# The boot of an attention and two-layer kernel: another order of fetches, passes and engines

## The chip, the cores and the metric

The program runs on one core of one Trainium2 chip. The metric is the device time of one execution in microseconds (us). A core has TensorE (PE; its weight loads are shown apart as PEld), VectorE (DVE), ScalarE (ACT), GpSimd (POOL) and SyncE (SP), which here issues the transfers. The engines run apart and wait for one another by semaphores.

## What is computed

The reference, cut to what matters: a linear attention with decay over 4 batches, 8 heads, 768 positions and head size 64; then a layer with a softmax-weighted activation and a norm; then a layer with a cosine.

```python
gamma = 1.0 - 2.0 ** (-5.0 - np.arange(H))
for t in range(S):
    state = gamma * state + einsum('bhd,bhe->bhde', k[:, :, t], v[:, :, t])
    y[:, :, t] = (1 / sqrt(D)) * einsum('bhd,bhde->bhe', q[:, :, t], state)
x = y.transpose(0, 2, 1, 3).reshape(B * S, H * D)         # 3072 tokens x 512
h = x @ w_in                                              # 512 x 1024
e = exp(h - max(h)); solu = h * e / (sum(e) + 1e-09)
ln = (solu - mean(solu)) / sqrt(var(solu) + 1e-06) * g_ln
x2 = ln @ w_out                                           # 1024 x 512
h2 = x2 @ w_in2; out = (h2 * cos(h2)) @ w_out2            # 512 x 2048 x 512
```

## The kernel before

**Attention.** The sequence is cut into 12 chunks of 64 positions, two batches at a time: 24 steps, each of which yields one tile of 128 tokens. `load` (L224) fetches for a step `dk` (k and q, 512 KB), `sv` (v and k, 512 KB) and `g` (decay factors, 128 KB), each into one of three buffers. GpSimd scales v by `kf` (L246). `attn(scores, outs)` (L281) then runs on TensorE: scores `sc` of one step (L257), the state `S` (L265) and the output `y` (L278) of the step before it. VectorE masks the scores to `M` (L311) and scales y by g to `x` (L324); ScalarE copies the state to `s` (L319).

**First layer.** Products are made in three passes of fp32r: each operand is split into a high part and the rest, and high x high, low x high and high x low are added up. `split` (L330) makes `xh` on ScalarE and `xl` on VectorE. The weights come as 64-bit words; `words` (L343) fetches a tile of them (`raw`) and turns it into fp32: one step on ScalarE (L353), three on VectorE (L357, L361, L366), a fourth one for the low word (L373). `w1` (L390) ends in `w1h` on ScalarE (L398) and `w1l` on VectorE (L401). w_in comes in five tiles: column half 0 in rows 0, 1 and 2 to 3 (two narrow tiles, 128x512, and a wide one, 128x1024), column half 1 in two wide tiles. `mm1(n, c)` (L456) makes h of token tile n, column half c, in 4 x 3 products (L471). `norm` (L478) reduces and scales h; `transp` and `mm2` (L527, L551) carry on to w_out, whose four tiles are converted by `o1` (L408).

**Order.** Nothing runs in the order in which it is written. `add` records an operation with its engine, cost, buffers and a due time; `Plan.order` (L97) replays engines and one wire (`MBUS`, in MB per us) and puts the operations out one after another; TensorE may pick among the next `LOOK` operations, the others by due time. The constants on top (L52 to L65) steer that. Each engine then runs its own instructions strictly in that order. `record` (L786) opens with the boot: tiles of w_in, the loads and the first attention steps by hand, then mm1 of tiles 0 and 1, and from tile 2 on a regular sequence of mm1, one attention step per tile, and w_out's conversion.

Of the kernel before, what the change touches and what calls it, by code (L numbers as in the profile page):

```python
# [22 lines left out]
C = 64  # L23
NI = S // C
# [40 lines left out]
B_LOAD = 0.0  # L65


class Plan:
# [28 lines left out]
    def order(self):  # L97
# [18 lines left out]
        at, sat, out = 0, 0, []  # L116
# [3 lines left out]
        while len(out) < n:  # L120
# [34 lines left out]
            free[e] = end  # L155
# [17 lines left out]
class Body:  # L173
# [48 lines left out]


    def load(self, n):  # L224
        bp, i = self.steps[n]
# [22 lines left out]
        self.add("POOL", 1.12, scale, w=[("v", sl)])  # L248
# [94 lines left out]
    def words(self, key, src, pool, slot, apart, wide=2):  # L343
# [40 lines left out]
        self.add("DVE", 0.15 + 0.55 * wide, low, r=[wk] if apart else [rk], w=[rk] if apart else [wk], bias=b)  # L384
# [5 lines left out]
    def w1(self, c, k, wide, slot):  # L390

        key = ("w1", c, k)
        rk, wk = self.words(key, self.pair("w_in1", k, slice(c * 1024, (c + 1) * 1024), wide), "boot", slot, True, wide)
# [6 lines left out]
        def low():  # L400
# [5 lines left out]
                 bias=self.bias)  # L406
# [144 lines left out]
    def mm2(self, g, p, look=1):  # L551
        for e in range(2):
            def go(e=e):
                if e == 0:
                    self.new("pst", ("y1", g), [128, 2, 256], F32, "y1")
                ds = slice((2 * p + e) * 128, (2 * p + e + 1) * 128)
                m = 0
                for j in range(K1):
                    lh, ll = self.t["lth", g, j // 2], self.t["ltl", g, j // 2]
                    for w, a in ((self.t["o1h"], lh), (self.t["o1l"], lh), (self.t["o1h"], ll)):  # L560
                        self.nc.tensor.matmul(out=self.t["y1", g][:, e], lhsT=w[:, j, ds], rhs=a[:, j % 2],  # L561
                                              start=(m == 0), stop=(m == 3 * K1 - 1))
                        m += 1
            self.add("PE", 2.88, go, r=[(w, f) for w in ("lth", "ltl") for f in range(4)]
# [432 lines left out]
```

## Time and profile before

| | us |
|---|---|
| median of three runs | 897.58 |
| lowest and highest | 897.24, 900.46 |
| the profiled execution, its own time | 900.29 |
| its span | 898.5 |
| TensorE busy | 876.3 (98%) |
| VectorE busy | 580.6 (65%) |
| ScalarE busy | 408.7 (45%) |
| GpSimd busy | 100.1 (11%) |

The span runs from the first to the last instruction on the core; what lies around it is in the profiled execution's time too. A busy TensorE is not TensorE at its peak: the records tell that it worked on something, and the granted clock beside it tells at which rate. The share of the whole span says little about a stage of it, so the rows further down are by stage.

### The profile page before, as it was taken

Reading aid. Unit: us, or ns where it says so; the run is one execution under the profiler, and the core shown is the slowest. Engines: PE = TensorE matmul, PEld = TensorE weight load, DVE = VectorE, ACT = ScalarE, POOL = GpSimd, SP = SyncE. Lnnn points to the kernel's source line nnn. Section 1 sums busy time; section 2 is a strip of 40 time slices with the busy share of each in tenths; the row PEclk is TensorE's granted clock in tenths of the full one; section 3 lists DMA queues with packets and bytes.
Section 4 is the critical chain, followed back from the end, with each engine's and each line's share of the span. In section 5 each row is a group of like instructions: output and inputs, shape, how many; then the busy total and the mean of one; then the engine's idle time right before and its main releaser. Section 6 shows DMA issues by size and latency. Waiting matters only on the chain.

```text
span 898.5 us, 16993 instructions
## 1 busy us (share of the span) xinstructions
PE 876.3 (98%) x7168; PEld 751.6 (84%) x7168; DVE 580.6 (65%) x849; ACT 408.7 (45%) x630; POOL 100.1 (11%) x200
## 2 busy tenths in 40 slices
PE   5799999999999999999999999999999999999997
PEld 4588899999999999988888888888888888888886
DVE  5899866658577565566666566556655665557553
ACT  3387665445454466453343344334433443334332
POOL 1254422223221221000000000000000000000000
PEclk9999999999999999999999999999999999999999
DMA  9766545676765264231030002000200020011002
GB/s 349 276 216 207 172 140 183 209 256 207 256 204 180 95 195 144 72 110 43 1 94 0 1 24 71 1 1 24 71 1 0 24 71 1 0 46 26 1 1 47
DMA packets 35852, 90.29 MB, mean 100 GB/s; under 512 B 4032, under 2 KB 13248, under 8 KB 35776
## 3 DMA queue, kind: packets, MB, share of 16 engines
q1 hardware_dynamic: 35344, 89.14, 30.4%
q8 instruction: 56, 0.92, 0.4%
q14 instruction: 20, 0.16, 0.1%
q10 hardware_dynamic: 432, 0.06, 0.0%
HBM read 68.22 MB, written 20.97 MB: 99 GB/s over the span
## 4 chain that ended last, share of the span: by engine, by line
PE 93%; DVE 4%; DMA 1%; issue 1%; ACT 0%; POOL 0%; SPq 0%; DVEq 0%; POOLq 0%
PE h L671 29%; PE acc L732 29%; PE y L561 16%; PE h L471 13%; PE tr L533 2%; PE sc L257 1%; PE y L278 1%; PE S L265 1%; DVE wt L366 1%; DMA sv<-vk_dram 1%; DVE raw L373 1%; DVE w1l L401 0%; DVE wt L357 0%; DVE wt L361 0%; DVE u L493 0%
## 5 line engine op out<-in xcount | busy, mean ns | idle before, releaser
L671 PE MATMUL h<-yh,w2h 128*128 128x512 f32 x384 | 149.5, 389 | 0.0
L671 PE MATMUL h<-yh,w2l 128*128 128x512 f32 x384 | 149.4, 389 | 0.0
L671 PE MATMUL h<-yl,w2h 128*128 128x512 f32 x384 | 149.4, 389 | 0.0
L732 PE MATMUL acc<-o2h,gh 128*128 128x512 f32 x384 | 149.4, 389 | 0.0
L732 PE MATMUL acc<-o2h,gl 128*128 128x512 f32 x384 | 149.4, 389 | 0.0
L732 PE MATMUL acc<-o2l,gh 128*128 128x512 f32 x384 | 149.4, 389 | 0.0
L692 ACT ACTIVATE r<-r,hp 128x512 f32<-128x512 f32 x96 | 69.5, 724 | 159.8 <-DVE r L689 159.8
L561 PE MATMUL y<-lth,o1h 128*128 128x256 f32 x384 | 110.0, 287 | 0.5 <-issue 0.5
L695 DVE TENSOR_TENSOR r<-r,h 128x512 f32<-128x512 f32 x96 | 65.9, 687 | 66.8 <-ACT r L692 66.8
L561 PE MATMUL y<-lth,o1l 128*128 128x256 f32 x384 | 108.6, 283 | 0.0
L561 PE MATMUL y<-ltl,o1h 128*128 128x256 f32 x384 | 108.6, 283 | 0.0
L681 DVE SCALAR_TENSOR_TENSOR r<-ki,h 128x512 f32<-128x512 int32 x96 | 65.9, 686 | 64.1 <-ACT ki L676 63.8
L703 DVE TENSOR_TENSOR gl<-r,gh 128x512 fp32r<-128x512 f32 x96 | 66.3, 690 | 45.8 <-ACT gh L699 45.6
L676 ACT ACTIVATE ki<-h 128x512 int32<-128x512 f32 x96 | 57.1, 595 | 79.6 <-PE h L671 79.6
L699 ACT ACTIVATE gh<-r 128x512 fp32r<-128x512 f32 x96 | 60.5, 630 | 55.3 <-DVE r L695 55.2
L671 PEld LDWEIGHTS h<-yl,w2h 128*128 128x128 f32 x384 | 72.1, 188 | 15.1
L732 PEld LDWEIGHTS acc<-o2h,gh 128*128 128x128 f32 x384 | 72.1, 188 | 15.0
L732 PEld LDWEIGHTS acc<-o2l,gh 128*128 128x128 f32 x384 | 72.0, 188 | 15.0
L732 PEld LDWEIGHTS acc<-o2h,gl 128*128 128x128 f32 x384 | 72.1, 188 | 14.9
L671 PEld LDWEIGHTS h<-yh,w2l 128*128 128x128 f32 x384 | 72.1, 188 | 14.8
L671 PEld LDWEIGHTS h<-yh,w2h 128*128 128x128 f32 x384 | 72.1, 188 | 14.8
L471 PE MATMUL h<-w1h,xh 128*128 128x512 f32 x192 | 78.8, 411 | 2.1 <-ACT w1h L398 1.4
(72 smaller groups left out, 1481.4 us busy)
## 6 DMA issues: line engine op xcount, KB each, us to landing
dk<-kq_dram SPq DMA_DIRECT2D x24, 512.0 KB, 4.6
sv<-vk_dram SPq DMA_DIRECT2D x24, 512.0 KB, 5.7
raw<-w_out_dram SPq DMA_DIRECT2D x12, 1024.0 KB, 6.8
raw<-w_in_dram SPq DMA_DIRECT2D x11, 1024.0 KB, 8.1
y1d<-ys SPq DMA_DIRECT2D x24, 256.0 KB, 2.7
yt<-y1d SPq DMA_DIRECT2D x24, 256.0 KB, 3.6
out_dram<-o SPq DMA_DIRECT2D x48, 128.0 KB, 2.4
kept_in<-wt SPq DMA_DIRECT2D x8, 512.0 KB, 4.7
```

The source lines that it names most:

```text
L257: self.nc.tensor.matmul(out=sc[r, j], lhsT=dk[r, 0, j], rhs=dk[r, 1, j], start=True, stop=True)
L471: self.nc.tensor.matmul(out=h[:, c], lhsT=a[:, k], rhs=w[:, k, cs], start=(k + m == 0), stop=(k == KD - 1 and m == 2))
L533: self.nc.tensor.transpose(out=tr[:, e, t * 128:(t + 1) * 128], in_=self.t["u", 2 * g + t].rearrange("p c f -> p (c f)")[:, j * 128:(j + 1 ...
L561: self.nc.tensor.matmul(out=self.t["y1", g][:, e], lhsT=w[:, j, ds], rhs=a[:, j % 2], start=(m == 0), stop=(m == 3 * K1 - 1))
L671: nc.tensor.matmul(out=h, lhsT=w[:, cs], rhs=a[:, k], start=(m == 0), stop=(m == 3 * KD - 1))
L676: nc.scalar.activation(out=T["ki", n, j], in_=T["h2", n, j], func=AF.Identity, scale=INV2PI, bias=0.25)
L681: nc.vector.scalar_tensor_tensor(out=r, in0=ki, scalar=-C1, in1=T["h2", n, j], op0=ALU.mult, op1=ALU.add)
L692: nc.scalar.activation(out=T["r", n, j], in_=T["r", n, j], func=AF.Sin, bias=self.hp[:, 0:1])
L695: nc.vector.tensor_tensor(out=T["r", n, j], in0=T["r", n, j], in1=T["h2", n, j], op=ALU.mult)
L699: nc.scalar.activation(out=T["gh", n, j], in_=T["r", n, j], func=AF.Copy)
L703: nc.vector.tensor_tensor(out=T["gl", n, j], in0=T["r", n, j], in1=T["gh", n, j].bitcast(F32), op=ALU.subtract)
L732: nc.tensor.matmul(out=T["acc", n, t], lhsT=a[:, ts_], rhs=w, start=(j == 0 and m == 0), stop=(j == K2 - 1 and m == 2))
```

## The change

The constants of the plan differ; the other parts, in the order of the diff:

- `warm`: 32 products of the identity with itself, written into the buffer of h of tile 0, as the first work of TensorE.
- `load`: g lies behind v and k in one transfer of 640 KB; for the steps in `V_ACT` ScalarE scales v in four instructions, one for each pair of heads, instead of GpSimd in one.
- `words` and `w1`: the two VectorE steps on the low words get a due time that is `B_LOW` later.
- `mm1` takes a range of passes, `(0, 2)`, `(2, 3)` or all; `mm2` is recorded in four pieces per output half instead of one.
- The constants tri, kf and g_ln come in one transfer `rows`.
- The boot is a list of words, `BOOT`: `w` a tile of w_in (column half, row, width, buffer), `L` a load, `s` scores, `a` an attention step, `x` a split, `m` products (tile, column half, rows from `PARTS`, passes).

```diff
-MBUS = 0.29
+MBUS = 0.40
+SHARE = 0.7
+EASE = 0.08
+WARM = 32
+V_ACT = (0, 2, 3, 7, 11, 12, 13)
-LOOK = 4
+LOOK = 3
...
-B_O1 = 16.0
-B_KEEP = 12.0
+B_O1 = 20.0
+B_KEEP = 6.0
...
-O1_AT = (1, 2, 4, 5)
+O1_AT = (2, 3, 4, 6)
...
+B_LOW = 24.0
+JOIN = 2
+PARTS = ((0,), (1,), (2, 3), (0, 1), (0, 1, 2, 3))
+BOOT = ("w:0010 w:0111 w:1023 L:0 L:1 s:0 a w:0222 x:0 L:2 s:1 a x:1 m:00002 a m:01302 m:10402 m:00102 a m:10423 a"
+        " m:00202 w:1224 m:00423 m:01202 m:01423:done m:11403:done x:2")
...
+            if e == "POOL" and ops[i][6] == "big":
+                if free["DVE"] > start:
+                    free["DVE"] += SHARE
+                else:
+                    owed = end
+            if e == "DVE" and start < owed:
+                end += SHARE
+                owed = 0.0
+            free[e] = end - (EASE if e in ("DVE", "ACT") else 0.0)
...
+    def warm(self):
+
+        t = self.new("ps1", ("warm",), [128, 2, 512], F32, "h")
+        for i in range(WARM):
+            self.nc.tensor.matmul(out=t[:, 0, 0:128], lhsT=self.ident, rhs=self.ident, start=True, stop=True)
...
         def sv():
-            t = self.new("att", ("sv", n), [128, 2, 8, C], F32, f"sv{sl}")
-            self.nc.sync.dma_start(out=t, in_=self.a["vk"][bp, i].rearrange("p (u j s) -> p u j s", u=2, s=C))
-
-        def g():
-            t = self.new("att", ("g", n), [128, NHP, C], F32, f"g{sl}")
-            self.nc.sync.dma_start(out=t, in_=self.a["c_g"][i].rearrange("p (a t) -> p a t", t=C))
+            t = self.new("att", ("svg", n), [128, 20 * C], F32, f"sv{sl}")
+            self.nc.sync.dma_start(out=t, in_=self.a["vk"][bp, i])
...
+        def scale_act():
+            v = self.t["sv", n][:, 0].rearrange("p (a b) e -> p a (b e)", b=2)
+            for a in range(NHP):
+                self.nc.scalar.activation(out=v[:, a], in_=v[:, a], func=AF.Copy, scale=self.kf[:, i, a:a + 1])
+
+        if n in V_ACT:
+            self.add("ACT", 1.60, scale_act, w=[("v", sl)])
+        else:
+            self.add("POOL", 1.12, scale, w=[("v", sl)], name="big")
...
-        self.add("DVE", 0.15 + 0.55 * wide, low, r=[wk] if apart else [rk], w=[rk] if apart else [wk], bias=b)
+        self.add("DVE", 0.15 + 0.55 * wide, low, r=[wk] if apart else [rk], w=[rk] if apart else [wk], bias=b + late)
...
-        if n == c == 0:
-            self.split(0)
-        if c == (n > 0) and n + 1 < NS:
+        if c == 1 and 1 < n < NS - 1:
             self.split(n + 1)
...
-                    for m, (a, w) in enumerate(((xh, self.w1h), (xl, self.w1h), (xh, self.w1l))):
+                    for m, (a, w) in list(enumerate(((xh, self.w1h), (xl, self.w1h), (xh, self.w1l))))[slice(*passes)]:
...
-            self.add("PE", 2.88, go, r=[(w, f) for w in ("lth", "ltl") for f in range(4)]
-                     + [(w, j) for w in ("o1h", "o1l") for j in range(K1)] + [("pool", "pst")], w=[("y1", e)], look=look,
-                     name=f"mm2 {g},{p},{e}")
+                self.add("PE", 0.72, go, r=[("lth", f), ("ltl", f), ("pool", "pst")] + ([("y1", 0)] if e else [])
+                         + [(w, 2 * f + i) for w in ("o1h", "o1l") for i in range(2)], w=[("y1", e)], look=look,
+                         name=f"mm2 {g},{p},{e},{f}")
...
-        nc.scalar.dma_start(out=self.tri, in_=self.a["c_tri"])
-        nc.scalar.dma_start(out=self.kf, in_=self.a["c_kf"].rearrange("p (a t) -> p a t", t=NHP))
-        nc.scalar.dma_start(out=self.gcol, in_=self.a["gln"])
+        nc.scalar.dma_start(out=rows, in_=self.a["c_rows"])
...
+        self.add("PE", 9.4, self.warm, w=[("h", 0, 0), ("h", 0, 1)], name="warm")
+        for word in BOOT.split():
+            kind, *arg = word.split(":")
```

What this does to the order shows best at three places. First TensorE, from the last attention rows of step 1 to the first products of h (`h<-w1h,xh` and its kin); before:

```order
L278 MATMUL y_247<-M1_239,sv1_125 64x64 x2
L278 MATMUL y_247<-dk1_123,s1_211 64x64 x16
L471 MATMUL h_294<-w1h_111,xh0_216 128x512
L471 MATMUL h_294<-w1h_111,xl0_243 128x512
L471 MATMUL h_294<-w1l_112,xh0_216 128x512
L471 MATMUL h_294<-w1h_111,xh0_216 128x512
L471 MATMUL h_294<-w1h_111,xl0_243 128x512
L471 MATMUL h_294<-w1l_112,xh0_216 128x512
L257 MATMUL sc_316<-dk2_131 64x64 x16
L471 MATMUL h_294<-w1h_111,xh0_216 128x512
L471 MATMUL h_294<-w1h_111,xl0_243 128x512
```

and now:

```order
L308 MATMUL y_270<-M1_259,sv1_154 64x64 x2
L308 MATMUL y_270<-dk1_152,s1_263 64x64 x16
L499 MATMUL h_328<-w1h_107,xh0_317 128x512
L499 MATMUL h_328<-w1h_107,xl0_325 128x512
L287 MATMUL sc_335<-dk2_158 64x64 x16
L499 MATMUL h_328<-w1h_107,xh0_317 128x512
L499 MATMUL h_328<-w1h_107,xl0_325 128x512
L499 MATMUL h_328<-w1h_107,xh0_317 128x512
L499 MATMUL h_328<-w1h_107,xl0_325 128x512
L287 MATMUL sc_371<-dk0_199 64x64 x2
L308 MATMUL y_374<-M0_366,sv2_160 64x64 x2
```

The products with w1l have left this place, and the scores of step 3 and the output of step 2 follow on the products with w1h.

Second VectorE, from its first instruction on; `wt0`, `raw0` and `wt1`, `raw1` are the two narrow tiles of w_in; before:

```order
L357 TENSOR_SCALAR wt0_135<-wt0_135 128x512
L361 TENSOR_SCALAR wt0_135<-wt0_135 128x512
L366 SCALAR_TENSOR_TENSOR wt0_135<-raw0_113,wt0_135 128x512
L373 SCALAR_TENSOR_TENSOR raw0_113<-raw0_113,wt0_135 128x512
L311 TENSOR_TENSOR M0_167<-sc_146,tri_66 128x512
L401 TENSOR_TENSOR w1l_112<-raw0_113,w1h_111 128x512
L324 TENSOR_TENSOR x0_207<-y_174,g0_119 128x512
L357 TENSOR_SCALAR wt1_205<-wt1_205 128x512
L361 TENSOR_SCALAR wt1_205<-wt1_205 128x512
L366 SCALAR_TENSOR_TENSOR wt1_205<-raw1_121,wt1_205 128x512
L373 SCALAR_TENSOR_TENSOR raw1_121<-raw1_121,wt1_205 128x512
L311 TENSOR_TENSOR M1_239<-sc_220,tri_66 128x512
```

and now:

```order
L387 TENSOR_SCALAR wt0_162<-wt0_162 128x512
L391 TENSOR_SCALAR wt0_162<-wt0_162 128x512
L396 SCALAR_TENSOR_TENSOR wt0_162<-raw0_142,wt0_162 128x512
L387 TENSOR_SCALAR wt1_166<-wt1_166 128x512
L403 SCALAR_TENSOR_TENSOR raw0_142<-raw0_142,wt0_162 128x512
L391 TENSOR_SCALAR wt1_166<-wt1_166 128x512
L431 TENSOR_TENSOR w1l_108<-raw0_142,w1h_107 128x512
L396 SCALAR_TENSOR_TENSOR wt1_166<-raw1_144,wt1_166 128x512
L403 SCALAR_TENSOR_TENSOR raw1_144<-raw1_144,wt1_166 128x512
L431 TENSOR_TENSOR w1l_108<-raw1_144,w1h_107 128x512
L341 TENSOR_TENSOR M0_197<-sc_177,rows_66 128x512
L387 TENSOR_SCALAR wt1_194<-wt1_194 128x1024
```

Both narrow tiles now go ahead of the first mask M0, and the first x, seventh before, is no longer among these rows.

Third SP's queue of transfers; before:

```order
L349 DMA raw0_113<-w_in1_dram 128x1024
L230 DMA dk0_115<-kq_dram 128x1024
L234 DMA sv0_117<-vk_dram 128x1024
L238 DMA g0_119<-c_g_dram 128x256
L349 DMA raw1_121<-w_in1_dram 128x1024
L230 DMA dk1_123<-kq_dram 128x1024
L234 DMA sv1_125<-vk_dram 128x1024
L238 DMA g1_127<-c_g_dram 128x256
L349 DMA raw2_129<-w_in1_dram 128x2x1024
L230 DMA dk2_131<-kq_dram 128x1024
L234 DMA sv2_133<-vk_dram 128x1024
L238 DMA g2_137<-c_g_dram 128x256
```

and now, from the second on (the first is `raw0` as before):

```order
L379 DMA raw1_144<-w_in1_dram 128x1024
L379 DMA raw3_146<-w_in1_dram 128x2x1024
L254 DMA dk0_148<-kq_dram 128x1024
L258 DMA sv0_150<-vk_dram 128x1280
L254 DMA dk1_152<-kq_dram 128x1024
L258 DMA sv1_154<-vk_dram 128x1280
L379 DMA raw2_156<-w_in1_dram 128x2x1024
L254 DMA dk2_158<-kq_dram 128x1024
L258 DMA sv2_160<-vk_dram 128x1280
L254 DMA dk0_199<-kq_dram 128x1024
L258 DMA sv0_319<-vk_dram 128x1280
L379 DMA raw4_321<-w_in1_dram 128x2x1024
```

Two more tiles of w_in stand ahead of dk0, g has gone, and raw4 stands behind the sv that takes buffer 0 for the second time.

## Rows read from the trace of the kernel before

**Rows 1.** busy time by stage; columns: stretch, length, busy time of each engine (instructions), clock, DMA

```profile
0.00:6.98 6.98, 0.00 (x1) 0.00 (x1) 0.73 (x2) 1.94 (x2) 0.76 (x8) 1.00 0.71 216
6.98:19.25 12.27, 9.20 (x225) 8.56 (x225) 8.15 (x13) 4.78 (x7) 2.92 (x3) 0.89 1.03 407
19.25:39.74 20.49, 14.50 (x323) 10.88 (x321) 20.11 (x22) 6.99 (x8) 4.88 (x4) 0.98 0.76 277
39.74:47.72 7.98, 7.55 (x145) 6.02 (x145) 4.79 (x7) 4.25 (x6) 0.66 (x3) 0.79 0.85 315
47.72:111.90 64.18, 64.04 (x1163) 53.09 (x1164) 59.26 (x77) 47.44 (x72) 34.69 (x73) 1.00 0.59 195
111.90:893.40 781.50, 780.97 (x5319) 673.02 (x5317) 487.13 (x730) 342.92 (x537) 56.20 (x111) 1.00 0.25 80
```

**Rows 2.** waits of TensorE up to 48 us; columns: in total, times, longest

```profile
PE sc L257 <- DMA dk<-kq_dram: 7.0, 1, 7.0
...
PE h L471 <- DVE w1l L401: 4.5, 3, 1.9
...
PE y L278 <- DVE M L311: 2.0, 1, 2.0
...
PE h L471 <- ACT w1h L398: 1.4, 1, 1.4
...
PE h L471 <- DVE u L493: 0.4, 1, 0.4
```

**Rows 3.** busy time from VectorE's first instruction to its last w1l

```profile
6.20:39.70 33.50, 23.70 (x544) 19.45 (x544) 28.95 (x36) 11.76 (x15) 7.80 (x6) 0.95 0.87 328
```

**Rows 4.** timeline of VectorE; columns: start, length, line, what, [idle before <- releaser]

```profile
6.68 0.43 DVE L361 TENSOR_SCALAR wt<-wt 128x512 int32<-128x512 int32 x1
...
7.14 0.69 DVE L366 SCALAR_TENSOR_TENSOR wt<-raw,wt 128x512 int32<-128x512 int32 x1
...
12.83 1.14 DVE L361 TENSOR_SCALAR wt<-wt 128x512 int32<-128x512 int32 x1
...
21.41 1.23 DVE L366 SCALAR_TENSOR_TENSOR wt<-raw,wt 128x1024 int32<-128x1024 int32 x1
...
27.60 1.95 DVE L366 SCALAR_TENSOR_TENSOR wt<-raw,wt 128x1024 int32<-128x1024 int32 x1
...
41.19 1.23 DVE L487 TENSOR_REDUCE sm<-h 128x1 f32<-128x1024 f32 x1 [0.90 <-PE h L471]
...
45.30 1.23 DVE L487 TENSOR_REDUCE sm<-h 128x1 f32<-128x1024 f32 x1 [2.29 <-PE h L471]
```

**Rows 5.** timeline of TensorE: the scores of steps 0 and 2

```profile
6.98 1.97 PE L257 MATMUL sc<-dk 64*64 64x64 f32 x32 [6.98 <-DMA dk<-kq_dram]
...
21.20 1.15 PE L257 MATMUL sc<-dk 64*64 64x64 f32 x32
```

**Rows 6.** chain of waits; columns: start, length, what

```profile
39.74 5.54 PE h L471 x16
...
53.45 0.20 PE sc L257 x2
...
55.48 5.67 PE h L471 x24
...
112.47 0.87 PE tr L533 x8
```

**Rows 7.** timeline of POOL: the identity, and v of steps 0 and 3

```profile
1.07 0.29 POOL masks.py:199 TENSOR_SCALAR_AFFINE_SELECT ident<-ident 128x128 f32<-128x128 f32 x1
...
8.45 1.04 POOL L246 TENSOR_TENSOR sv<-sv,kf 128x512 f32<-128x512 f32 x1 [7.08 <-DMA sv<-vk_dram]
...
27.16 1.30 POOL L246 TENSOR_TENSOR sv<-sv,kf 128x512 f32<-128x512 f32 x1 [7.48 <-DMA sv<-vk_dram]
```

**Rows 8.** timeline of ScalarE: one narrow and one wide instruction

```profile
7.86 0.63 ACT L398 ACTIVATE w1h<-wt 128x512 fp32r<-128x512 f32 x1 [1.68 <-DVE wt L366]
...
17.96 1.12 ACT L353 ACTIVATE wt<-raw 128x1024 f32<-128x1024 f32 x1
```

More of the change, by code (lines that the diff above doesn't have):

```diff
@@ L340, in split, with words @@
         self.add("DVE", 0.70, low, r=[("x", n % RING), ("xh", n % 2)], w=[("xl", n % 2)])
-    def words(self, key, src, pool, slot, apart, wide=2):
+    def words(self, key, src, pool, slot, apart, wide=2, late=0.0):
         rk = ("raw", pool, slot)
@@ L392, in w1 @@
         key = ("w1", c, k)
-        rk, wk = self.words(key, self.pair("w_in1", k, slice(c * 1024, (c + 1) * 1024), wide), "boot", slot, True, wide)
+        rk, wk = self.words(key, self.pair("w_in1", k, slice(c * 1024, (c + 1) * 1024), wide), "boot", slot, True, wide, B_LOW)
         cs = slice(c * 512, (c + 1) * 512)
@@ L464, in go @@
             def go(ks=ks):
-                if c == 0 and ks[0] == 0:
+                if ("h", n) not in self.t:
                     self.new(pool, ("h", n), [128, 2, 512], F32, "h")
@@ L469, in go @@
                 for k in ks:
-                    for m, (a, w) in enumerate(((xh, self.w1h), (xl, self.w1h), (xh, self.w1l))):
+                    for m, (a, w) in list(enumerate(((xh, self.w1h), (xl, self.w1h), (xh, self.w1l))))[slice(*passes)]:
                         self.nc.tensor.matmul(out=h[:, c], lhsT=a[:, k], rhs=w[:, k, cs], start=(k + m == 0),
                                               stop=(k == KD - 1 and m == 2))
-            self.add("PE", 0.68 * len(ks) + 0.03, go, r=[("xh", n % 2), ("xl", n % 2), ("pool", pool)]
-                     + [(w, c, k) for w in ("w1h", "w1l") for k in ks], w=[("h", hb, c)], look=look, name=f"mm1 {n},{c}")
-        if c == 1:
+            need = [("xh", n % 2), ("pool", pool)] + ([("xl", n % 2)] if passes[0] < 2 and passes[1] > 1 else [])
+            need += [("w1h", c, k) for k in ks if passes[0] < 2] + [("w1l", c, k) for k in ks if passes[1] > 2]
+            self.add("PE", 0.227 * len(ks) * (passes[1] - passes[0]) + 0.03, go, r=need, w=[("h", hb, c)], look=look,
+                     name=f"mm1 {n},{c},{passes}")
+        if c == 1 and done:
             self.norm(n, hb)
@@ L762, in setup @@
         self.hp = hp.tile([128, 120], F32, name="hp")
-        self.tri = const.tile([128, C], F32, name="tri")
-        self.kf = const.tile([128, NI, NHP], F32, name="kf")
-        self.gcol = const.tile([128, K1], F32, name="gcol")
+        rows = const.tile([128, C + NI * NHP + K1], F32, name="rows")
+        self.tri = rows[:, 0:C]
+        self.kf = rows[:, C:C + NI * NHP].rearrange("p (a t) -> p a t", t=NHP)
+        self.gcol = rows[:, C + NI * NHP:]
         self.mhalf = const.tile([128, 8], F32, name="mhalf")
@@ L832, in record @@
         oq = [(0, "stg", 0), (1, "stg", 1), (2, "boot2", 0), (3, "stg", 0)]
-        self.mm1(0, 1, ((0, 1), (2, 3)), look=look)
-        for n in range(1, 2 * EARLY):
+        for n in range(2 * EARLY):
             if n > 1:
@@ L926, in body @@
 @with_exitstack
-def body(ctx: ExitStack, tc: tile.TileContext, kq, vk, c_g, c_tri, c_kf, w_in1, w_out1, gln, w_in2, w_out2, out):
-    b = Body(ctx, tc, kq=kq, vk=vk, c_g=c_g, c_tri=c_tri, c_kf=c_kf, w_in1=w_in1, w_out1=w_out1, gln=gln,
-             w_in2=w_in2, w_out2=w_out2, out=out)
+def body(ctx: ExitStack, tc: tile.TileContext, kq, vk, c_rows, w_in1, w_out1, w_in2, w_out2, out):
+    b = Body(ctx, tc, kq=kq, vk=vk, c_rows=c_rows, w_in1=w_in1, w_out1=w_out1, w_in2=w_in2, w_out2=w_out2, out=out)
     b.setup()
```

85 lines of the change are left out of this document (41 added, 44 removed).

## The prediction

> **What bounds the kernel now.** I read the busy time by stage first [rows 1]. From 47.72 us on TensorE is busy 64.04 of 64.18 us, and then 780.97 of 781.50: nothing is to be had there. Before that it is idle 6.98 + 3.07 + 5.99 + 0.43 = 16.5 us. I call 47.72, where the first product of h for token tile 2 starts, the mark; what follows it is a dense stream, so the kernel ends earlier by as much as the mark comes earlier, plus the TensorE work that is already done at the mark and was not before. The waits of TensorE [rows 2] say what the idle time is: 7.0 until the first dk has landed, 4.5 for the low part of w_in1 (w1l, on VectorE), 2.0 for a mask, 1.4 for w1h, and 0.4 at the mark itself. Last, VectorE in the stretch that ends with the last w1l (39.68): it is busy 28.95 of 33.5 us [rows 3]. So VectorE, converting w_in1 from 64-bit words, is the bound of the boot, and every w1l in it holds the three-pass products behind.
>
> **The passes split, and VectorE's new order.** The same five tiles of w_in1 are converted with the same 25 instructions. Before, TensorE needed a tile's w1l for its third product; now the xh and xl products against w1h run for tiles 0 and 1 first, and the w1l products later. So w1l is no longer what TensorE waits for, until the last one. VectorE's count from its start (6.2) to the last w1l: 35 instructions before, 36 now (five masks and two xl as before, four x instead of three). Its pure work before is 28.95 less the stretch that POOL causes. While POOL scales v, a VectorE instruction next to it takes 1.14 instead of 0.43, or 1.95 instead of 1.23 [rows 4]; there are four such in this stretch, two of which are shown, together 2.5 us. So 28.95 - 2.5 = 26.4, and with one x more (0.69 long, 0.6 of it before the next starts) 27.0.
>
> What it waits for now. Before M0 stand the ten instructions of the two narrow tiles: 2 x (2 x 0.43 + 3 x 0.69) = 5.9 us [rows 4], so it reaches M0 at 12.1. M0 needs sc0, and sc0 needs dk0 and the end of the idle products (both below: 11.1 and 11.9); sc0 takes 1.15 us at the faster pace [rows 5]; M0 can start at 13.2, a wait of 1.1. Nothing later is late by my count: x0 needs y0, which runs after sc1 (dk1 lands at 14.1) from 15.3 to 16.4, and VectorE reaches x0 at 17.1; x1 needs y1 at about 19.2, reached at 21. Of POOL's products three (steps 1, 4, 5) still lie in the stretch: 3 x 0.7 = 2.1 (0 to 3). Sum: 6.2 + 27.0 + 1.1 + 2.1 = 36.4 for the last w1l, 3.3 earlier than 39.7. Bounds: 34.3 without any stretch, 39.7 if all is eaten.
>
> TensorE between: the first product needs xl0, which VectorE finishes at 6.2 + 5.9 + 1.1 + 6.2 = 19.4 (eight instructions from M0 to xl0, six of at most 0.69 and two of 1.23 [rows 4], 6.6, less some 0.4 by which records overlap). Up to the last w1l it has 34 products of 0.236 (24 in 5.67) = 8.0, sc2 with 1.15, and the attention steps (3,2), (4,3), (5,4) with 2.03 each (55.48 - 53.45) = 6.1 [rows 5, 6]: 15.3 us, done at 34.7 if never held. That leaves 1.7 us of cover under VectorE. Behind the last w1l come 14 products (3.3), the attention step (6,5) (2.0), and the gap of 0.4 [rows 2]: 36.4 + 5.8 = 42.2 for the mark, 5.5 earlier, and with one attention step (2.03) more done than before: 7.5 us.
>
> **w_in1 fetched first.** Three tiles of it (2.10 MB) now go ahead of dk0 on SP's queue, so dk0 is behind 2.62 MB instead of 1.05. Before, sv0 had landed at 8.35 with 1.57 MB issued up to it, and the sv of step 3 at 27.1 with 8.78 MB [rows 7]: 0.385 MB per us. dk0 then lands at 8.35 + 1.05/0.385 = 11.1, four us later than before; sv0 at 12.8, sv1 at 15.9. This is the cost of the reorder, and it is already in the 1.1 us wait above. The last w_in1 tile (raw4) lands with 8.91 MB at 27.4; ScalarE's first step on it takes 1.12 [rows 8]; VectorE reaches it at about 29: no wait, with half a us of cover.
>
> **Constants, g with v.** Three constant transfers become one and 24 g transfers vanish into v's. SP's issues shrink; the bytes stay: nothing. But the buffer of v is now held until x has read g, so SP's fetch of sv for step 3 waits for x0, and raw4 and all later fetches stand behind it in SP's queue. By the times above x0 ends at 17.8, and raw4, issued then, is limited by the bytes ahead of it, not by the wait. Zero here; a us late for each us that x0 ends after some 18.5.
>
> **Idle products.** 32 products of the identity need only the identity (made from 1.07 on, in 0.29 [rows 7]). A transpose of 128 columns takes 0.109 (8 in 0.87) [rows 6]; an fp32 product has two such records, 64 in all: 7.0 us at the faster pace and 13.9 at half of it, so they end between 8.5 and 15.4. I take the middle, 11.9, because the stretch must start at the lower pace: sc0 took 1.97 before, right after idling, against 1.15 for the same 32 records later [rows 5]. They cost 0.8 against dk0 (11.1), in the 1.1 above; from 0 to 4.3. The Trainium skill (TensorE: Matmul & The Clock Gate, Part 1) has it that the default state is throttled and activity releases the throttle; the trace's two durations of sc agree. By that rule sc0 and sc1 run at the faster pace; without it sc0 would end 0.8 us later, and so would the sum.
>
> **v on ScalarE.** Seven of the 24 steps leave POOL (1.04 to 1.30 each [rows 7]) for four ScalarE instructions on 128 columns. From 1.12 for 1024 and 0.63 for 512 columns [rows 8] I take 0.14 + 0.12 = 0.26 each, 1.05 a step; at most 4 x 0.63 = 2.5. Step 0 alone is on the path: v landed at 12.8, scaled at 13.9, wanted by TensorE at 15.3: hidden, and barely so at 2.5. ScalarE has room after the mark (47.44 of 64.18 [rows 1]). The Trainium skill (ScalarE: Activation LUTs, Rules for kernel authors) budgets about 0.3 us per ACTIVATE and 0.83 ns per element; by that a step takes 1.6, an estimate from that page, and the sum is the same.
>
> **The rest.** mm2 in quarters and the planner's new constants move rows in a stretch where TensorE waits 0.14 + 0.53 us in all [rows 1]: 0, between -0.5 and +1.
>
> **Does the rest keep the lead?** VectorE's lead at the last w1l is 3.3 + 0.6 = 3.9; before, its reductions of h of tiles 0 and 1 then waited 0.9 and 2.3 us for TensorE [rows 4], which falls away: 7.1 at the mark. From the mark to 111.9 it is busy 59.26 of 64.18 [rows 1], 4.9 of slack, so it can follow. I take back 0.5. Net 7.0.
>
> **Rivals.** (1) The lead is given back: if VectorE keeps only the 3.9, because norm and w_out1 steps bunch up, the time is 897.58 - 3.9 = 893.7. For it: VectorE is at 92% after the mark. Against: fewer POOL products beside it. (2) More than forecast: no stretch and early products give a last w1l at 34.3, a lead of 9.1: 888.5. (3) The slow one: the lower clock. TensorE still has gaps (13.1 to 14.2, about 16.4 to 17.1), and before, after the waits for w1l, 16 products from 39.74 took 5.54 us instead of 3.8 [rows 6], the clock of that stage being 0.79 [rows 1]: partly the lower of its two levels, 1.2 GHz. If it is low from the first product to the last w1l, 15.3 us of work become 1.97/1.15 = 1.7 times as long: + 10.7, less 1.7 of cover, = 9.0, and the time is 899.6. If the idle products run low throughout too, M0 is 3.5 later: 903.1, slower. It turns against the change from 7.0 us of such loss on; a fall over a third of the stretch gives about 893 to 895. (4) The split does not do what it says: if tile 0's products still wait for other operands (xl0, w1h), TensorE's 34 products come late and the cover of 1.7 is gone; each us beyond that is one lost, 893 for 4 us.
>
> **The numbers.** The profiled execution took 900.29, its span 898.5 with 1.8 around it; like for like the changed kernel's would be 893.3. The three runs have a median of 897.58, 2.7 below it; 897.58 - 7.0 = 890.6. If this loss from 39.74 on is the profiled run's own, the lead is about 1.7 smaller: 892.3, inside the forecast's own range, 888.9 to 893.0. Chances: forecast 0.60, (2) 0.12, (1) and (4) 0.12, (3) in part 0.10, (3) whole 0.06. 0.5%, about what a measurement here can tell from no change, is 4.5 us: faster is below 893.1. Faster 0.60 + 0.12 = 0.72; same 0.22; slower 0.06. The range 888.0 to 895.0 leaves out (3) beyond a third and the edge of (2).
>
> **What would show it.** Right: the first sc at 11 to 12.5; VectorE without a wait over 0.5 us from M0 to the last w1l, which ends at 35 to 38; TensorE waiting for w1l once or twice, under 2 us together; the first h of tile 2 at 41 to 44 with the attention step (6,5) before it; no wait of TensorE over 1 us after that. Wrong: idle products ending after 14; a granted clock near 0.5 between 20 and 37 us; raw4's first step starting after 30; a chain after the mark that runs through VectorE to about 100, with TensorE waiting there.

## The result

The changed kernel takes 905.38 us (median of 5 runs, 903.85 to 908.18), the kernel before 898.69 beside it: ratio 1.008, 95% interval 1.0053 to 1.0108. It is slower by 0.8%, some 7 us, where I had forecast 7 us faster. The profiled execution took 903.95 (span 902.0), against 900.29 (898.5) before; the other 3 us are in runs that were not profiled.

The stages of the changed kernel, cut at the events of [rows 1] (first sc, first product of h, the end of TensorE's last wait ahead of the mark, the mark, then the first product of h of token tiles 10 and 23); columns as there:

```profile
0.00:11.68 11.68, 10.26 (x64) 10.14 (x64) 4.84 (x10) 3.83 (x6) 0.76 (x8) 1.00 0.81 283
11.68:21.45 9.77, 5.58 (x225) 5.15 (x225) 8.53 (x11) 6.11 (x10) 1.25 (x1) 1.00 1.02 420
21.45:40.06 18.61, 15.02 (x445) 12.12 (x443) 15.28 (x17) 7.82 (x15) 2.92 (x3) 1.00 0.75 279
40.06:49.16 9.10, 8.67 (x150) 6.90 (x150) 4.93 (x7) 3.63 (x7) 1.26 (x4) 0.81 0.71 248
49.16:108.44 59.28, 59.28 (x1025) 49.18 (x1025) 53.75 (x72) 49.73 (x84) 27.10 (x61) 1.00 0.61 204
108.44:329.93 221.49, 218.16 (x2677) 200.62 (x2673) 139.68 (x180) 111.08 (x166) 56.31 (x108) 0.99 0.56 190
```

The same two late stages of the kernel before (tile 2 to 10, tile 10 to 23):

```profile
47.72:109.45 61.73, 61.59 (x1152) 51.06 (x1152) 56.98 (x74) 44.99 (x69) 32.97 (x67) 1.00 0.60 198
109.45:326.18 216.73, 216.26 (x2677) 199.44 (x2673) 140.50 (x180) 110.45 (x165) 54.05 (x107) 1.00 0.58 195
```

The loss has two places. The boot gave 1.0 us by tile 10 (108.44 for 109.45) instead of 7, and tiles 10 to 23 lost 4.8 (221.49 for 216.73) instead of nothing. Behind them the kernels run alike (572.1 and 572.3 us).

TensorE's waits, up to 120 us and behind (columns as in [rows 2]):

```profile
PE y L308 <- issue: 4.9, 4, 2.4
PE S L295 <- POOL sv L267: 1.6, 1, 1.6
...
PE sc L287 <- DVE wt L387: 1.4, 1, 1.4
...
PE y L592 <- issue: 3.0, 2, 1.8
PE y L592 <- DVE ltl L574: 0.3, 1, 0.3
```

Of [rows 2] the waits for w1l and w1h are gone, as forecast, and the 7.0 us for the first dk lie under the idle products. (The 1.4 put down to wt ends at 14.19, where the forecast had the second dk land, 14.1.) In their place stands "issue", 4.9 + 3.0 us, which before was 0.5: the engine waited for nothing that the profile shows. The rows of these stalls (TensorE's timeline; start, length, what, [idle before]):

```profile
19.80 0.27 PE L308 MATMUL y<-M,sv 64*64 64x64 f32 x1 [1.27 <-issue]
...
25.73 0.27 PE L308 MATMUL y<-M,sv 64*64 64x64 f32 x1 [0.84 <-issue]
...
30.77 0.27 PE L308 MATMUL y<-M,sv 64*64 64x64 f32 x2 [0.39 <-issue]
...
37.48 0.22 PE L308 MATMUL y<-dk,s 64*64 64x64 f32 x1
40.06 0.27 PE L308 MATMUL y<-dk,s 64*64 64x64 f32 x1 [2.37 <-issue]
...
191.36 0.28 PE L592 MATMUL y<-lth,o1l 128*128 128x256 f32 x1 [1.82 <-issue]
...
258.51 0.27 PE L592 MATMUL y<-lth,o1h 128*128 128x256 f32 x1 [1.20 <-issue]
```

The last in the boot parts two records of one and the same float32 product: no operand can be late there. Two things mark these places. They lie 127 to 128 product records apart, counted in the trace, or a multiple of it; each record has a weight load beside it, so that is some 256 instructions. And ahead of each stands one packet of 16 KB (256 x 64 bytes) on q8, a DMA queue for instructions, here for the first, the last in the boot, and the one at 191 (lines of the DMA view for the tenth of a microsecond from 17.5, 37.7 and 189.0):

```profile
q8 instruction: 1, 0.02, 57.6%
...
q8 instruction: 1, 0.02, 55.8%
...
q8 instruction: 1, 0.02, 58.4%
```

Packets at 17.5, 23.3, 28.4, 37.7 and 189.0; TensorE goes on at 19.80, 25.73, 30.77, 40.06 and 191.36, each 2.3 to 2.4 us later. (One more in the boot, at 32.7, came without a stall.) I call such a packet a refill. That q8 feeds TensorE the whole program shows: its number of packets follows TensorE's number of product records, 7168 in the kernel before, 8832 in e5, 4960 in e10 (runs further down), which is 127 to 128 records for each packet. Lines of their pages, in this order:

```profile
q8 instruction: 56, 0.92, 0.4%
...
q8 instruction: 69, 1.13, 0.5%
...
q8 instruction: 39, 0.64, 0.3%
```

An attention step is 128 records in 2.03 us [rows 6], so it uses up a whole refill in less than the 2.3 us that pass behind a packet. In the kernel before, the packets at 14.8, 21.0 and 31.3 fell into or just ahead of TensorE's waits for data (14.1 to 16.1, 22.3 to 23.8, 32.3 to 34.2):

```profile
16.08 0.27 PE L278 MATMUL y<-M,sv 64*64 64x64 f32 x2 [2.00 <-DVE M L311]
...
23.78 0.50 PE L471 MATMUL h<-w1h,xh 128*128 128x512 f32 x1 [1.44 <-ACT w1h L398]
...
34.17 0.50 PE L471 MATMUL h<-w1l,xh 128*128 128x512 f32 x1 [1.87 <-DVE w1l L401]
```

The clock adds to it. Granted clock (column behind the last bracket) behind the boot's last stall and behind the stall of 191, then at the boot's last stall in run e15, which is described below:

```profile
41.71:45.12 3.41, 3.41 (x9) 0.50 0.84 309
191.90:195.31 3.41, 3.41 (x18) 0.50 0.44 172
...
40.81:49.00 8.19, 7.37 (x150) 1.00 0.78 306
```

After each of the two stalls of 2 us the clock stands at 0.50, the lower level (1.2 GHz), for 3.4 us. It does not follow on every such stall: in e3 and e15 TensorE stalls at the same place for 3.0 and 2.9 us and the clock stays at 1.00. Nor is the first of the two falls a difference between the kernels, since the kernel before has one at the same point of its boot, behind its waits for w1l [rows 1, rows 6]. Tiles 13 to 15 took 39.0 us for 35.4 before: 2.0 of it the stall, 1.6 the clock.

### The profile page after: what moved, and what is told of

It reads as the page before. It is cut to its first block, busy times and chain, and to the rows that moved or that the text cites. A ratio compares the mean times of both kernels' runs of the same rounds, so it can differ in the third digit from the quotient of the medians.

```text
span 902.0 us, 17109 instructions
## 1 busy us (share of the span) xinstructions
PE 884.3 (98%) x7232; PEld 759.6 (84%) x7232; DVE 575.6 (64%) x849; ACT 418.1 (46%) x658; POOL 92.5 (10%) x193
## 4 chain that ended last, share of the span: by engine, by line
PE 95%; DMA 2%; DVE 1%; issue 1%; SPq 0%; ACT 0%; POOL 0%; ACTq 0%; POOLq 0%
PE h L701 29%; PE acc L762 29%; PE y L592 15%; PE h L499 14%; PE tr L563 2%; PE sc L287 2%; PE y L308 2%; PE S L295 1%; DMA sv<-vk_dram 1%; DMA raw<-w_out_dram 1%; DVE sm L517 0%; DVE ltl L574 0%; SPq L254 0%; POOL sv L267 0%; SPq L379 0%
## 5 line engine op out<-in xcount | busy, mean ns | idle before, releaser
L762 PEld LDWEIGHTS acc<-o2h,gl 128*128 128x128 f32 x384 | 72.1, 188 | 14.8
L701 PEld LDWEIGHTS h<-yh,w2h 128*128 128x128 f32 x384 | 72.0, 188 | 14.8
```

Of the source, the lines that this page charges most:

```text
L701: nc.tensor.matmul(out=h, lhsT=w[:, cs], rhs=a[:, k], start=(m == 0), stop=(m == 3 * KD - 1))
L762: nc.tensor.matmul(out=T["acc", n, t], lhsT=a[:, ts_], rhs=w, start=(j == 0 and m == 0), stop=(j == K2 - 1 and m == 2))
```

## The experiments

Theory A: TensorE runs out of instructions. Rivals: B, transfers of dk and v and their scaling; C, the clock alone; D, the new order of the middle costs by itself. All runs but e5, which was run once for its trace, stand in one table: median time, ratio to the kernel before on the same chip, when the profiled execution reached token tiles 2 (the mark), 10 and 23, and TensorE's "issue" up to 120 us and behind.

| run | us | ratio (95%) | tile 2 | tile 10 | tile 23 | issue |
|---|---|---|---|---|---|---|
| before | 898.69 | | 47.72 | 109.45 | 326.18 | 0, 0.5 |
| after | 905.38 | 1.008 (1.0053-1.0108) | 49.16 | 108.44 | 329.93 | 4.9, 3.0 |
| e1_idle48 | 912.13 | 1.015 (1.0137-1.0163) | 58.64 | 119.53 | 337.68 | 2.7, 0 |
| e2_idle24 | 905.42 | 1.0077 (1.0064-1.009) | 48.61 | 110.26 | 329.41 | 6.3, 1.1 |
| e3_boot_alone | 901.85 | 1.0034 (1.0022-1.0047) | 48.24 | 108.69 | 324.65 | 4.2, 0 |
| e4_rest_alone | 905.66 | 1.0075 (1.0063-1.0087) | 45.83 | 108.35 | 329.96 | 0.7, 1.0 |
| e6_halves_lookahead | 915.24 | 1.0185 (1.0162-1.0209) | 49.59 | 113.15 | 338.56 | 5.5, 0 |
| e7_before_halves | 905.65 | 1.0081 (1.0067-1.0094) | 46.12 | 111.43 | 331.40 | 1.2, 0 |
| e8_halves_in_order | 916.31 | 1.0198 (1.018-1.0216) | 51.29 | 114.86 | 340.69 | 2.2, 0 |
| e9_after_few | 881.20 | 0.982 (0.9797-0.9842) | 40.94 | 93.78 | 305.59 | 0, 0 |
| e10_before_few | 886.07 | 0.9869 (0.985-0.9888) | 45.70 | 106.83 | 310.53 | 0, 0 |
| e11_early_dk | 902.35 | 1.0047 (1.0026-1.0067) | 46.35 | 107.52 | 327.94 | 1.1, 1.4 |
| e12_rest_few | 895.72 | 0.9967 (0.9952-0.9983) | 43.73 | 100.32 | 321.77 | 0, 0 |
| e13_early_dk_old_rest | 897.79 | 0.9987 (0.9975-0.9999) | 46.45 | 107.36 | 323.51 | 1.6, 0.3 |
| e14_mm2_whole | 909.45 | 1.0112 (1.0098-1.0127) | 49.17 | 109.86 | 331.78 | 5.9, 3.1 |
| e15_old_constants | 902.98 | 1.0038 (1.0023-1.0052) | 48.92 | 109.67 | 327.01 | 7.6, 1.1 |
| e16_boot_few | 881.07 | 0.9796 (0.9779-0.9813) | 41.13 | 100.17 | 304.16 | 0, 0 |

**Other instructions ahead, same work.** Two kernels differ from the changed one in the idle products alone, which shifts every later refill in the program.

```diff
-WARM = 32                      # products of 128 columns
+WARM = 48                      # e1: rhs=self.ident[:, 0:64]
+WARM = 24                      # e2: rhs=self.ident[:, 0:96], twice (192 columns)
```

> The changed kernel with 48 idle products of 64 columns in place of 32 of 128: about the same idle time (10 us), 64 more TensorE instructions (a product is two records and two weight loads) ahead of everything else; no other instruction is moved. Theory A (TensorE runs out of instructions: its 16 KB refills on queue q8 come once in some 256 instructions, and an attention step burns 256 in 2.0 us): all refill boundaries shift 32 product records earlier in the program, so the stalls marked issue move to other places: in the boot about 3.6 us of them instead of 4.9, none between the halves of y<-dk,s at 37.7; first product of token tile 2 near 46.5 us instead of 49.2, the time 900 to 904 (the later boundaries move too, by an amount I can't tell). Theory B (transfers of v and dk and their scaling make the wait): nothing moves, 905 and the mark at 49.2 within 0.5. Theory C (clock): nothing moves, since the idle time is the same.

> The changed kernel with 24 idle products of 192 columns in place of 32 of 128: about the same idle time, 32 TensorE instructions fewer ahead of everything else; nothing else is moved. Theory A: the refill boundaries shift 16 product records later in the program; worked through with the boundaries read off the trace they then fall into stretches of short products five times in the boot, some 7 us of issue stalls, the mark near 50.5 us (49.2 before), 905 to 909. Theories B and C: 905 and the mark at 49.2 within 0.5.

e1's expectation fell with its premise: 96 records of 64 columns took 20.7 us, not 10, so its boot starts 10 us late and tells nothing on the mark. Its middle does: with the same order, tiles 10 to 23 took 218.15 us without an issue stall, for 221.49 with 3.0. In e2 the idle products end 0.6 us later, and two stalls of 0.8 us stand near where they stood (20.1 and 26.1); but the 2.4 us at 40.1 are gone, and 4.0 us stand at 48.2, between two records of S. So B and C, by which nothing moves, fall; but three stalls up to the mark where I expected five, and the time is that of the changed kernel.

More than the times, the counts tell. Windows of TensorE from 0 to just ahead of a stall, first two of the changed kernel, then three of e2 (the number of product records is in brackets):

```profile
0.00:19.79 19.79, 14.18 (x222) 1.00 0.90 339
0.00:25.72 25.72, 19.27 (x349) 1.00 0.93 357
...
0.00:20.12 20.12, 15.03 (x222) 1.00 0.91 340
0.00:26.06 26.06, 20.11 (x349) 1.00 0.93 358
0.00:48.19 48.19, 38.27 (x858) 1.00 0.83 308
```

With 16 idle records fewer ahead of it, e2 stalls behind the same 222 and 349 records, and so at other products. The next stalls stand behind 731 records in the changed kernel, e3, e14 and e15, behind 858 in e2, e3 and e15, behind 477 in e1, behind 223 and 351 in e5: within two records the 222 and a multiple of 127 to 128. The stall belongs to the count of instructions and not to what is computed there.

**The refill by itself.** Behind the idle products stand 800 more, of the attention's shape, that wait for nothing.

```diff
+        for i in range(400):
+            for r in self.half:
+                self.nc.tensor.matmul(out=t[r, 0, 0:64], lhsT=self.ident[r, 0:64], rhs=self.ident[r, 0:64], ...)
```

> The changed kernel with 800 more idle products behind the 32, of the attention's shape (64 x 64, alternating between the two halves of the rows, 2 records each) on the identity matrix: they wait for no data. The boot's loads run beside the first of them and then stop, since nothing reads their buffers, so DMA is busy up to about 20 us and quiet after. Theory A: the records come in groups of 127 with a stall marked issue behind each; a group takes 2.0 us; a 16 KB packet on q8 stands 2.35 us ahead of each resumption; while DMA is quiet the stall is 0.3 + 0.1 + 2.35 - 2.0 = about 0.7 us (0.5 to 1.2), while DMA is busy 2 to 4 us. Rivals (stalls come from the attention's data or buffers): an even stream without stalls, 1600 records in 25 us.

TensorE's timeline of that run, and its windows (stretch, length, busy time of PE, PEld, DVE, ACT, POOL, clock, DMA share, GB/s):

```profile
10.96 4.88 PE L247 MATMUL h<-ident 64*64 64x64 f32 x159
17.17 3.94 PE L247 MATMUL h<-ident 64*64 64x64 f32 x128 [1.33 <-issue]
22.82 38.48 PE L247 MATMUL h<-ident 64*64 64x64 f32 x1313 [1.70 <-issue]
...
14.00:18.00 4.00, 2.67 (x92) 2.54 (x90) 0.00 (x0) 0.11 (x1) 1.04 (x1) 1.00 1.02 416
18.00:22.00 4.00, 3.12 (x107) 2.98 (x104) 0.00 (x0) 0.00 (x0) 0.00 (x0) 1.00 0.48 197
22.00:26.00 4.00, 3.18 (x109) 3.18 (x110) 0.00 (x0) 0.00 (x0) 0.00 (x0) 1.00 0.01 4
...
30.00:40.00 10.00, 10.00 (x350) 10.00 (x348) 0.00 (x0) 0.00 (x0) 0.00 (x0) 1.00 0.02 5
```

The 128 records between the two stalls took 3.94 us, not the 2.0 I expected, and still TensorE stalled 1.70 behind them: with DMA full, refill follows refill after 22.82 - 17.17 = 5.65 us. Once DMA is quiet, the packets come every 3.4 to 3.6 us (20.5, 23.9, 27.4, 31.0), which is the pace at which these slower records (0.029 us each) use them up, and 1313 records run without a stall. So A holds for products that wait for no data, and beside the loads a refill takes two microseconds more than the 3.6 that are enough without them. How short it can be on a quiet DMA is not shown, nor whether an attention step at 0.016 us a record would run without a stall there. In the boot of the changed kernel TensorE went on 5.9 and 5.0 us after it last had (19.80, 25.73, 30.77). That the packet stands behind data on its DMA engine fits this; it is not shown.

**The parts.** e3 holds the new boot and the old rest, e4 the old boot and the new rest; e14 and e15 undo one half of the rest each.

```diff
 e3, and e15 without its last line; from the end of the boot on:
-MBUS, SHARE, EASE, LOOK, B_O1, B_KEEP = 0.40, 0.7, 0.08, 3, 20.0, 6.0
+MBUS, SHARE, EASE, LOOK, B_O1, B_KEEP = 0.29, 0, 0, 4, 16.0, 12.0
-O1_AT = (2, 3, 4, 6); V_ACT = (0, 2, 3, 7, 11, 12, 13)
+O1_AT = (1, 2, 4, 5); V_ACT = (0, 2, 3)
+mm2 in one piece, as before (alone in e14)
```

> The new boot alone: everything up to the remaining 14 products of the first two token tiles as in the changed kernel (idle products, transfers, split passes, v of steps 0, 2, 3 on ScalarE), but from there on mm2 in one piece, the planner's constants, look-ahead and v on GpSimd of the kernel before. Theory A: the mark stays at 49.2 with 4.9 us of issue stalls; the instruction count is that of the changed kernel and so are the refill boundaries, and the later loss of 4.1 us stays for the most part, 903 to 906. Theory D (the reordered middle costs by itself): the later 4.1 us go, 900 to 902.

> The rest alone: the boot of the kernel before, and from the end of the boot on mm2 in quarters, constants, look-ahead and v of steps 7, 11, 12, 13 on ScalarE as in the changed kernel. Theory A: instructions ahead of the middle are those of the kernel before, so the refills fall as before, 897 to 900 with hardly any issue stalls. Theory D: the later 4.1 us come, 901 to 903.

> The changed kernel with mm2 in one piece again, all constants new. Theory A: the later loss is where refill boundaries meet attention steps, which both the quarters and the constants move: anything from 899 to 906, with the difference from the changed kernel equal to that of the issue stalls behind the mark and the time at the lower clock behind each. Theory D: if the quarters cost by themselves, 900 to 902 without a change in those stalls.

> The changed kernel with mm2 in quarters, but from the end of the boot on the constants, look-ahead and v on GpSimd of the kernel before. Theory A: as for mm2 in one piece, 899 to 906, in step with the issue stalls. Theory D: if the constants cost by themselves, 900 to 902.

e3's middle took 215.96 us, no longer than before, so the later loss comes with the rest, as D has it, and not with the instruction count, as A had it. (The profiled execution is the fastest of e3's eight, 898.49 for a median of 901.85; by medians the boot alone costs some 3 us.) The rest alone is as slow as both together (e4, 905.66) and slower than either theory had it; 1.0 us of it is issue behind 120 us; its largest single loss is a wait for data at the first transposes, which the changed kernel doesn't have:

```profile
113.20 0.41 PE L553 MATMUL tr<-ident,u 128*128 128x128 f32 x2 [1.83 <-DVE u L513]
```

Undoing the quarters alone made it worse (909.45, beyond both expectations). The stall near 190 us is longer there, once more 2.4 us behind a packet (191.4):

```profile
193.82 0.39 PE L591 MATMUL y<-ltl,o1h 128*128 128x256 f32 x1 [3.13 <-issue]
```

But that is not where e14 loses: of the 4.5 us by which its profile is longer than the changed kernel's, 1.4 lie ahead of tile 10, 0.4 between tiles 10 and 23, and 2.6 behind tile 23, 1.5 of them a wait for ltl. Undoing the constants alone gave 2.4 us back (902.98) with more issue, 8.7 us for 7.9. So the time does not go in step with the issue stalls, as A had it for both, and neither half has a price of its own that adds up.

In the profile of the changed kernel the two stalls (3.3 against the usual pitch) and the clock behind the first (1.6), less a stall of 0.6 that the kernel before has in these tiles, are 4.3 of the 4.8; of e4's 4.9 in the same tiles 1.0 is issue, 2.4 waits for u and ltl, and the rest I can't assign.

**Fewer instructions.** Each attention step issues 32 products of 128 x 128 in one pass for 64 of 64 x 64 in two: 32 records for 128. Tiles, waits and transfers stay; the products mix a pair's neighbours, so the values are not the reference's.

```diff
-        for r in self.half:
-            self.nc.tensor.matmul(out=sc[r, j], lhsT=dk[r, 0, j], rhs=dk[r, 1, j], start=True, stop=True)
+        a = 2 * (j // 2)      # top(): the upper 16 bits of each word, as bfloat16
+        self.nc.tensor.matmul(out=sc[:, j], lhsT=self.top(dk[:, 0, a:a + 2] ...), rhs=self.top(dk[:, 1, j]), ...)
```

> The changed kernel with each attention step as 32 products of 128 x 128 on the upper halves of the words (bfloat16) in place of 64 of 64 x 64 in float32: a quarter of the instructions, every tile, wait and transfer as it is; the products mix the neighbours of a pair, so the output isn't the reference's. Theory A (TensorE's instruction supply): no issue stalls are left, the mark comes 5 to 7 us before that of the same edit on the kernel before, and this kernel is 5 to 8 us faster than that one, as the prediction had said of the change itself. Theory B (data) and Theory C (clock): this kernel stays 5 to 8 us slower than the same edit on the kernel before.

> The kernel before with the same edit of the attention's products (32 of 128 x 128 on the upper halves of the words for 64 of 64 x 64), output not the reference's: the control of the run with the changed kernel. Theory A: it gains little beyond what the cheaper products themselves give (22 steps by the difference of a step from 2.03 us, which the run shows), since its refills lay under waits for data; its waits for dk (7.0) and w1l (4.5) stay.

> The new boot alone (rest as in the kernel before) with each attention step as 32 products of 128 x 128 on the upper halves of the words, output not the reference's. To be set against the kernel before with the same edit (886.1). Theory A: without a shortage of instructions the boot's gain that the prediction worked out (7.0) returns: 876 to 881. If the boot has another bound (data): 884 to 888.

> The run with the rest of the change alone (boot of the kernel before, mm2 in quarters, new constants from the end of the boot on), with the same edit of the attention's products as in the two runs above; output not the reference's. Theory A (its 7 us are issue stalls that the new order has moved onto attention steps): it stands within 1.5 us of the same edit on the kernel before. Theory D (the order costs by waits for data): it stays 4 us or more above it.

No issue stall is left in any of the four. The changed kernel is now 4.9 us faster than its control (881.20 for 886.07; 4.4 by the ratios), where it had been 6.7 slower. Its new boot alone (e16) reaches tile 10 at 100.17 for 106.83 and is 5.0 us faster by medians, 0.9869 - 0.9796 = 0.7% or 6.6 us by the ratios. The mark comes at 41.13 for 45.70, one attention step ahead. All of this lies at the lower edge of what A expected, or just short of it. TensorE's waits up to 60 us, of the control and of e16:

```profile
PE sc L260 <- DMA dk<-kq_dram: 7.5, 2, 6.9
PE S L268 <- POOL sv L246: 4.0, 2, 2.0
PE h L473 <- ACT w1h L400: 3.7, 2, 2.6
PE h L473 <- DVE w1l L403: 3.6, 3, 1.5
```

```profile
PE sc L290 <- DMA dk<-kq_dram: 4.5, 2, 2.3
PE h L501 <- DVE u L525: 2.4, 2, 1.5
PE S L298 <- ACT s L351: 2.3, 1, 2.3
...
PE h L501 <- DVE w1l L433: 0.5, 1, 0.5
```

That is the boot the prediction described: the long wait for dk and the waits for w1l are gone, and nothing as long takes their place. By B and C both pairs should have kept the order of the real kernels.

The edit changes more than the number of instructions: a step takes 0.98 us for 2.03, so TensorE has less work in the boot too. That the stalls go with the instructions is shown; that all of the boot's gain comes back by that alone is not. An estimate from the real kernel points the same way: the three stalls before 37.5 us cost 1.5, 1.0 and 0.6 us from record to record, so without them TensorE would have reached its last attention record near 34.4, ahead of VectorE's last w1l (36.98).

e12 went against A: the rest alone stays 9.6 us above its control, and the waits that grew are for VectorE (tr for ltl 5.6 us where the control has 1.1, h for xl 3.7 where it has none). The size isn't that of the real kernel: the shorter step makes TensorE wait for VectorE more, and the mean granted clock of the profiled execution is 0.990 for 0.996, which is worth up to 5 us. Nor does it hold behind the new boot: e9 and e16 differ in the rest alone and take 881.20 and 881.07. So the new order of the middle has a cost beside A, but only behind the old boot is it clear of noise once the stalls are gone, and why, the runs do not show.

**Two mends that failed, one that came out level.** If the stall needs a run of short products, cut the run: attention steps in two halves with products of h between.

```diff
-                self.mm1(n, 1, look=look)
-                attend()
+                attend(0)
+                self.mm1(n, 1, look=look)
+                attend(1)
```

> The changed kernel with each attention step of 128 records cut into two halves of 64, with products of the token tiles between them (in the middle the second half of mm1; in the boot where the planner puts it); the work is the same. Theory A: a stretch of 127 records can no longer be short products alone, so the issue stalls behind the mark go (3.3 us and the 1.65 us that the lower clock costs behind them) and those in the boot shrink from 4.9 to some 2 to 3: 895 to 899. Theory D (the middle's order costs by itself): 903 to 906, since the order of everything else stays.

> As the run with halves and look-ahead, but TensorE's boot goes exactly in the written order, so that each half has products of a token tile behind it there too. Theory A: issue stalls in the boot 1 to 2 us in all instead of 4.9, the mark 2 to 4 us earlier if no wait for w1l takes their place: 892 to 898. Theory B (data): stalls turn into waits for data of the same size, the mark stays at 48 to 50: 898 to 901 at best.

> The kernel before with the same halving of its attention steps from the end of its boot on. Theory A: it has one issue stall of 0.6 us behind the boot, which goes: 897 to 899, no difference that counts. If halving is faster by itself, whatever the stalls: 893 to 896.

All three are far off. Behind 120 us the issue stalls did go, but a token tile with halves takes 8.08 us for 7.69 (tiles 3 to 4 of e7 and of before): one more change from long products to short and back costs 0.39 us. From tile 2 to tile 23 the halves cost 6.8 us in e7 and 8.2 in e6. In the boot the stalls stayed (5.5 and 2.2).

The other mend leaves the steps whole and starts the refills earlier: dk and sv of the first steps ahead of the second and third w_in1 tile, as before, and 16 idle products.

```diff
-BOOT = ("w:0010 w:0111 w:1023 L:0 L:1 s:0 a w:0222 x:0 ...
+BOOT = ("w:0010 L:0 w:0111 L:1 s:0 a w:1023 w:0222 x:0 ...
-WARM = 32
+WARM = 16
```

> The changed kernel with the first four transfers in the order of the kernel before (first dk and sv behind the first w_in1 tile, not behind three of them) and 16 idle products in place of 32, which end about when the first dk lands: all else in the written order. Theory A: the attention's first two steps start near 7 us instead of 11.7, so the refill that the idle time did not need is asked for earlier and two of the boot's four stalls fall into waits for data; w_in1's last tile comes where it came; the mark 2 to 4 us earlier, 900 to 903. Theory B: the last w1l comes at the same time, and the mark stays within 1 us, 904 to 906.

> The new boot alone (rest as in the kernel before), with the first transfers in the order of the kernel before and 16 idle products: the two edits that each took about 3 us off the changed kernel, together. If both act on different stretches (refills of the boot, order of the middle): 897 to 900, level with the kernel before. If both gains are luck with where the refills fall: 900 to 905.

With the new rest (e11) it gives back 3 us, the mark comes 2.8 us earlier, and the issue up to 120 us shrinks from 4.9 to 1.1, as A had it; with the old rest (e13) it is at 897.79, ratio 0.9987: better than both kernels by the interval, and by less than a measurement here can tell from no change. Its boot has 1.6 us of issue, but waits for u (2.4) at the mark.

## Why the prediction was wrong

- **The bound of the boot** was read right as far as it goes. VectorE's last w1l ran from 35.75 to 36.98 (forecast 36.4), busy 27.96 us from 6.20 on [rows 3]; M0 started at 12.88 after a wait of 0.55; TensorE no longer waits for w1l. That the end came within 0.6 us is partly luck: VectorE was busy 1.1 us less than the 29.1 forecast (27.0 + 2.1) and waited 2.8 us in all instead of 1.1.
- **Loads, idle products, v on ScalarE** came as worked out. The first sc started at 11.68 (forecast 11.9) and took 1.15, the faster of the two values of [rows 5]: by the rule cited (TensorE: Matmul & The Clock Gate, Part 1, in the Trainium skill) that was to be so, and the trace agrees: the first 28 idle records took about 0.21 us each, the later ones 0.11. In e1 it does not: 20.7 us of idle products of 64 columns ran at 0.21 to their end, and the first sc behind them took 1.97. (The column of the granted clock reads 1.00 in all of these stretches, so only the durations tell.) The four ScalarE steps took 1.28 us (forecast 1.05; the estimate from the Trainium skill, ScalarE: Activation LUTs, Rules for kernel authors, was 1.6).
- **The step that failed** is "TensorE between: ... 15.3 us, done at 34.7 if never held". First product 21.45 for 19.4, and from there to 40.06 TensorE was busy 15.02 of 18.61 us, but with 28 of the 34 products, sc and the three steps, which the prediction prices at 13.9: the work was some 1 us too cheap, and the "never held" was wrong. TensorE, not VectorE, bounded the boot. I priced an attention step at 2.03 us from a stretch where 24 long products stand between two steps [rows 6], and set such steps closely behind each other, under a full DMA. In e5 a refill of 128 records takes 5.65 us under a full DMA. The mark missed 42.2 by 7.0 us: the four stalls are 5.7 from record to record ("issue 4.9" is the idle time alone), and the lower clock behind them 1.6 (20 products took 6.4 us, the usual pitch is 0.236); the 1.7 of cover took up some, and the remaining 1.3 I put down, without a test, to changes between short and long products and a later start. With the instructions cut, a gain came, 4.4 to 6.6 of 7.0 us, in kernels whose steps are also shorter.
- **"The rest: 0, between -0.5 and +1"** was mis-sized: 4.8 in the profiled run. That TensorE waits little in a stretch does not say that a new order keeps it so.
- **The rivals.** (3), the lower clock, was right as a mechanism and wrong in place and cause: the clock was 1.00 up to 40.06, and fell behind the stalls. (4) comes nearest in form, TensorE's products late though VectorE is early; its cause was not an operand. None of the four had instructions for a resource, though q8 stood in the profile's list of DMA queues.

## What to carry to other kernels

Instructions are a stream with a rate: here 256 of them, 128 product records, took 5.7 us to refill beside full loads and 3.6 or less without, and an attention step used them up in 2.0. Before packing short products into the waits of a boot, ask what those waits also cover, and count the engine's instructions as well as its time. Where a profile says "issue" inside a run of short products, look for the 16 KB packet ahead of it and count the records up to it. Here padding moved such stalls (e1, e2), an earlier start of the attention shrank them (e11, e13), and fewer instructions removed them (e9, e10, e12, e16).

## What the runs showed of the hardware

- From the packet on q8 to the next instruction of TensorE 2.3 to 2.5 us passed, in the boot, at 191 and 258 us, and in e5.
- One more change from 128x512 products to 64x64 ones and back cost TensorE 0.39 us (8.08 for 7.69 us a tile).
- 96 idle records of 64 columns took 20.74 us, 64 of 128 columns 10.33. With 128 columns the first 28 took about 0.21 us each and the rest 0.11; with 64 columns all took 0.21. Why these never came to the faster pace, no run shows.
- Stalls of 2.4 and 1.8 us (changed kernel) were followed by a granted clock of 0.50; stalls of 3.0 and 2.9 us (e3, e15) were not.
- Open: when the next refill is asked for (from one resumption in the changed kernel's boot to the next packet 2.0 to 5.6 us passed), and how the stalls are spread over runs that were not profiled; e3's eight runs lie between 898.49 and 903.87.
